# Sinkhorn-MoE behind banded attention: 1024-token blocks, with weight operands kept in DRAM after the first pass

## The chip, the cores and the metric

One core of a Trainium2 chip. The metric is device time in microseconds for one execution, the median of three runs. TensorE (PE) multiplies, VectorE (DVE), ScalarE (ACT) and GpSimd (POOL) work on its results and on its operands, and SyncE (SP) issues the DMA transfers.

## The reference

```python
scores = scale * np.matmul(q, k.transpose(0, 1, 3, 2)) + bias        # B 4, H 8, S 768, D 64
scores = np.where(keep, scores, -1000000000.0)                       # 8 global keys, 96 local
attn_out = softmax(scores) @ v
x = attn_out.transpose(0, 2, 1, 3).reshape(3072, 512)
P = np.exp(x @ w_gate - max)                                         # 8 experts
for _ in range(8):
    P /= P.sum(1, keepdims=True) + 1e-09
    P /= P.sum(0, keepdims=True) + 1e-09
    P *= N / E
for e in range(E):
    h = np.maximum(x @ w1[e], 0.0)                                   # w1[e]: 512 x 1024
    out += P[:, e:e + 1] * (h @ w2[e])                               # w2[e]: 1024 x 512
```

Every expert sees every token. All values are float32. The kernel writes a float32 operand as a high and a low part (`xh`, `xl`; `wh`, `wl`), so one product of 128 x 128 by 128 x n takes three matmuls: hi by lo, lo by hi, hi by hi.

## The kernel before

*Attention stage.* `Banded.unit` works on 8 units of 384 tokens, each with four head pairs, and leaves the result in `xh`, `xl` (the last write of a head pair is L390). Beside it runs a filler, `background`: the gate of a finished unit and its first `NF0 = 4` F-tiles (128 of the 1024 hidden columns each) of expert 0, by plain matmuls: layer 1 in `h_ps`, layer 2 in `y_ps`, whose result goes to `y_spill`. `between` doles it out over the attention's slots. The filler of the last unit comes after attention has ended, and `sinkhorn` is woven into it and the first steps.

*Block stage.* The remaining work is 30 groups, each two F-tiles of one expert, on four blocks of 768 tokens (two units each): 120 steps. `layer1_strassen` makes layer 1 of a block from seven products instead of eight, 42 matmuls 384 wide, in the banks `c`, `d`, `a`, `b`. `second` is layer 2, plain: 36 matmuls of 512 into `y_ps` for six token tiles, and for each tile a DVE operation (L944) that scales by the gate's weight `pm` and adds to `acc`. Layer 2 of a step stands in the program behind layer 1 of the next.

*Operands.* The seven token operands of a block (`right_operands`, `right_sums`, `right_difference`) are sums of x quarters; `combine` makes one with POOL (or POOL, DVE and ACT where `hurry` is set). The weight operands of a group are made once per half: SP loads `w1f` and `w2f` (512 KB each), POOL makes five sums `wsum` (L565), ACT copies the high parts (L542) and POOL subtracts the low ones (L543).

*Order.* The four blocks are worked in two halves of two, so all 30 groups' weights are prepared twice; x and the sums of the first two blocks wait in DRAM (`x_spill`, `s_spill`) and come back by `reload`. A scheduler orders the instructions of each engine, except where `keep_in_program_order` (class `InOrder`, L83, L86) holds PE's matmuls to the program: in attention, and in the block stage from the second expert on. All DMA transfers go through SP's queue.

## Time and profile before

| | us |
|---|---|
| median of three runs (2239.43 to 2240.81) | 2239.45 |
| profiled execution, first to last instruction | 2239.4 |
| PE busy | 2215.1 (99%) |
| DVE busy | 1388.3 (62%) |
| POOL busy | 791.7 (35%) |
| ACT busy | 693.3 (31%) |
| mean granted PE clock, share of full speed | 0.993 |
| moved by DMA | 133.74 MB, 60 GB/s over the span |

The span of the profiled execution is the device time within 0.1 us, so there is next to nothing around it. Busy shares are averages over two different stages: attention with filler up to about 340 us, and blocks from there to 2234. PE's durations overlap (a matmul's 0.4 us of 512 columns starts before the one ahead has ended), so work on PE is counted by starts.

### The profile page before, as it was taken

How to read it: one execution, taken by the hardware profiler on the slowest of the kernel's cores; microseconds unless marked ns; L12 is line 12 of the kernel's file. 1: busy time of each engine (PE TensorE's matmuls, PEld its weight loads, DVE VectorE, ACT ScalarE, POOL GpSimd, SP SyncE). 2: the span in 40 equal slices, each digit the busy share in tenths (PEclk: the TensorE clock that was granted, in tenths of full speed). 3: DMA queues.
4: the chain of work that ended last, by engine and by line, in shares of the span. 5: the costliest groups of instructions: out<-in, count | busy, mean ns of one | idle time of the engine just before them, and what ended most of it. 6: DMA issues, size and time to landing. Idle time of an engine off the chain costs nothing.

```text
span 2239.4 us, 31408 instructions
## 1 busy us (share of the span) xinstructions
PE 2215.1 (99%) x12147; PEld 1984.8 (89%) x12147; DVE 1388.3 (62%) x2682; ACT 693.3 (31%) x1592; POOL 791.7 (35%) x655
## 2 busy tenths in 40 slices
PE   8999999999999999999999999999999999999999
PEld 5888888989999899998999989989999899998997
DVE  5555557866666666666666666666666666666665
ACT  6677663232222222222222133222222222222221
POOL 5257356333333333323333234332333333333320
PEclk8999999999999999999999999999999999999999
DMA  7466432101101011010110551111011110111001
GB/s 167 127 181 170 120 97 66 37 30 38 38 29 34 33 38 38 29 38 29 38 38 29 188 188 39 38 30 37 29 39 38 34 33 29 38 38 38 29 20 58
DMA packets 177614, 133.74 MB, mean 60 GB/s; under 512 B 117040, under 2 KB 148784, under 8 KB 177456
## 3 DMA queue, kind: packets, MB, share of 16 engines
q1 hardware_dynamic: 177456, 131.65, 19.6%
q8 instruction: 97, 1.59, 0.3%
q14 instruction: 61, 0.50, 0.1%
HBM read 108.81 MB, written 22.81 MB: 59 GB/s over the span
## 4 chain that ended last, share of the span: by engine, by line
PE 92%; POOL 3%; ACT 2%; issue 2%; DVE 1%; DMA 0%; SPq 0%; ACTq 0%; DVEq 0%; POOLq 0%
PE y_ps L83 44%; PE bank_c L83 11%; PE bank_d L83 11%; PE bank_a L83 11%; PE bank_b L83 5%; PE h_ps L83 2%; PE t_ps L86 1%; PE s_ps L83 1%; PE o_ps L83 1%; PE tp L86 1%; ACT p_sb L296 1%; PE y_ps L690 1%; PE y_ps L692 0%; PE y_ps L691 0%; POOL xsum L615 0%
## 5 line engine op out<-in xcount | busy, mean ns | idle before, releaser
L944 DVE SCALAR_TENSOR_TENSOR acc<-y_ps,pm,acc 128x512 f32<-128x512 f32 x672 | 502.9, 748 | 260.7 <-PE y_ps L83 259.4
L83 PE MATMUL y_ps<-w2l,hh 128*128 128x512 f32 x1476 | 578.0, 392 | 0.0
L83 PE MATMUL y_ps<-w2h,hh 128*128 128x512 f32 x1476 | 576.9, 391 | 0.0
L83 PE MATMUL y_ps<-w2h,hl 128*128 128x512 f32 x1476 | 576.5, 391 | 0.0
L543 POOL TENSOR_TENSOR w2l<-w2f,w2h 128x1024 fp32r<-128x1024 f32 x60 | 144.4, 2406 | 646.6 <-ACT w2h L542 646.6
L83 PEld LDWEIGHTS y_ps<-w2h,hh 128*128 128x128 f32 x1476 | 276.9, 188 | 58.3
L83 PEld LDWEIGHTS y_ps<-w2h,hl 128*128 128x128 f32 x1476 | 277.1, 188 | 53.8
L83 PEld LDWEIGHTS y_ps<-w2l,hh 128*128 128x128 f32 x1476 | 277.2, 188 | 53.5 <-issue 0.2
L543 POOL TENSOR_TENSOR wl<-wsum,wh 128x1280 fp32r<-128x1280 f32 x60 | 177.9, 2964 | 350.6 <-ACT wh L542 350.6
L565 POOL TENSOR_TENSOR wsum<-w1f 128x256 f32<-128x256 f32 x300 | 213.4, 747 | 218.4 <-DMA w1f<-in_moe_w_dram 218.4
L630 ACT ACTIVATE hh<-bank_b 128x384 fp32r<-128x384 f32 x120 | 59.1, 492 | 399.8 <-DVE bank_b L670 396.2
L542 ACT CAST w2h<-w2f 128x1024 fp32r<-128x1024 f32 x60 | 63.2, 1053 | 380.9 <-PE y_ps L83 357.3
L663 ACT COPY t<-bank_c 128x384 f32<-128x384 f32 x120 | 57.8, 482 | 360.6 <-PE bank_c L83 353.9
L665 DVE TENSOR_TENSOR t<-t,bank_d 128x384 f32<-128x384 f32 x120 | 66.5, 554 | 165.6 <-PE bank_d L83 162.7
L83 PE MATMUL bank_c<-xh,wh 128*128 128x384 f32 x460 | 155.2, 337 | 0.0
L83 PE MATMUL bank_c<-xl,wh 128*128 128x384 f32 x460 | 154.9, 337 | 0.0
L83 PE MATMUL bank_c<-xh,wl 128*128 128x384 f32 x460 | 154.5, 336 | 0.0
L83 PE MATMUL bank_d<-xl,wh 128*128 128x384 f32 x460 | 153.8, 334 | 0.3 <-DVE hl L631 0.3
L83 PE MATMUL bank_d<-xh,wl 128*128 128x384 f32 x460 | 153.6, 334 | 0.0
L83 PE MATMUL bank_d<-xh,wh 128*128 128x384 f32 x460 | 153.6, 334 | 0.0
L83 PE MATMUL bank_a<-sl,wh 128*128 128x384 f32 x460 | 153.6, 334 | 0.0
L83 PE MATMUL bank_a<-sh,wl 128*128 128x384 f32 x460 | 153.6, 334 | 0.0
(219 smaller groups left out, 3986.6 us busy)
## 6 DMA issues: line engine op xcount, KB each, us to landing
w1f<-in_moe_w_dram SPq DMA_DIRECT2D x62, 512.0 KB, 3.5
w2f<-in_moe_w_dram SPq DMA_DIRECT2D x62, 512.0 KB, 3.6
out_dram<-acc SPq DMA_DIRECT2D x24, 256.0 KB, 2.2
ys<-y_sb SPq DMA_DIRECT2D x21, 256.0 KB, 2.1
acc<-ys SPq DMA_DIRECT2D x7, 768.0 KB, 5.1
acc<-in_q_dram SPq DMA_DIRECT2D x32, 96.0 KB, 2.6
acc<-in_k_dram SPq DMA_DIRECT2D x32, 96.0 KB, 2.5
acc<-in_v_dram SPq DMA_DIRECT2D x32, 96.0 KB, 2.3
```

The lines of the kernel that those rows point to most:

```text
L83: return self.tc.keep_in_program_order(self.engine.matmul(*args, **kw))
L86: return self.tc.keep_in_program_order(self.engine.transpose(*args, **kw))
L296: nc.scalar.activation(out=pv, in_=pv, func=AF.Exp, bias=mx[:, u:u + 1], scale=-1.0, accum_out=sm[:, i, j:j + 1])
L542: self.nc.scalar.copy(out=hi, in_=full)
L543: self.nc.gpsimd.tensor_tensor(out=lo, in0=full, in1=hi, op=ALU.subtract)
L565: nc.gpsimd.tensor_tensor(out=s[:, n], in0=x, in1=y, op=op)
L630: nc.scalar.activation(out=hh, in_=src, func=AF.Relu)
L663: nc.scalar.copy(out=t3, in_=c)
L665: tt(out=t3, in0=t3, in1=d, op=ALU.subtract)
L690: self.pe.matmul(y_ps, lhsT=hh[:, cols], rhs=lf, start=(f == 0), stop=False)
L944: nc.vector.scalar_tensor_tensor(out=a, in0=y_ps, scalar=moe.pm[:, tt, e:e + 1], in1=a, op0=ALU.mult, op1=ALU.add)
```

## The change

Blocks of 1024 tokens take the place of those of 768: three blocks, and every matmul of a block is 512 wide. `NF0` is 2, so the filler does the first two F-tiles of expert 0, and 31 groups are left. `layer1_fast` is a seven-product form with other sums (`FIRST`; four banks `x`, `y`, `z`, `w`).

Pass 1 works the third block while it makes the weights' operands. `make_group` makes for each group seven operands of w1 (four of them sums, `left_sums`) and seven of w2, and stores them in DRAM (`w1s`, `w2s`, 1.84 MB each). Layer 2 is plain there (48 matmuls).

Passes 2 and 3 work the first and second block. They make no weights: `load_first` and `load_second` read the operands back (`w1r`, `w2r`). Layer 2 has seven products too (`SECOND`, 42 matmuls into `m_ps`): class `Fast` scales the hidden values by the gate's weight (`pbc`, a row broadcast from DRAM), and makes the seven operands `hop` from them with POOL and ACT. The results of the products are added up over 29 groups in seven tiles `m` (128 x 1024) in SBUF by DVE (L1225), and are turned into output tiles once a pass: seven adds (L1229 to L1235), then in group 29 (`PLAIN`) 64 transposes in all `c_ps2` bring them to `acc` (L1253). The last two groups of a pass have layer 2 plain. The x operands of the first two blocks are stored as they are made, in pieces, and read by `load_x` (seven tiles of 1 MB, `xr`) ahead of a pass.

```diff
-NF0 = 4
+NF0 = 2
+HB = 4
+BT = 2 * HB
+BU = HB * P
+OPS = ("s1", "s2", "s3", "s4", "a11", "a12", "a22")
+FIRST = (("p1", "x", "a11", "b11", True), ("p6", "y", "s2", "t2", True), ("p2", "x", "a12", "b21", False),
+         ("p5", "z", "s1", "t1", True), ("p7", "w", "s3", "t3", True), ("p3", "z", "s4", "b22", False),
+         ("p4", "w", "a22", "t4", False))
+SECOND = (("p1", "a11", "b11"), ("p3", "s4", "b22"), ("p5", "s1", "t1"), ("p7", "s3", "t3"), ("p6", "s2", "t2"),
+          ("p2", "a12", "b21"), ("p4", "a22", "t4"))
...
-    def strassen_stage(self, e, f, stage):
...
+    def make_group(self, staged, pool, spool, stage, dst1, dst2, dst2p):
+
+        nc, KH, HD = self.nc, self.KH, self.DM // 2
+        s, w1f, w2f = staged
+        w = pool.tile([P, 7, 2, KH * P], F32R, name="w1ops")
+        v = pool.tile([P, FG * 2, 2, HD], F32R, name="w2ops")
+        self.split(w[:, 4:6, 0], w[:, 4:6, 1], w1f[:, :, 0:P].rearrange("p (o c) f -> p o c f", o=2))
+        self.split(w[:, 0:4, 0], w[:, 0:4, 1], s.rearrange("p o c f -> p o (c f)"))
+        self.split(w[:, 6, 0].rearrange("p (c f) -> p c f", f=P), w[:, 6, 1].rearrange("p (c f) -> p c f", f=P), w1f[:, KH:, P:])
+        for f, n in enumerate((slice(0, 4, 3), slice(1, 3))):
+            self.split(v[:, n, 0], v[:, n, 1], w2f[:, f].rearrange("p (e d) -> p e d", e=2))
+        nc.sync.dma_start(out=dst1.bitcast(F32), in_=w.bitcast(F32))
+        if dst2p is not None:
+            nc.sync.dma_start(out=dst2p.bitcast(F32), in_=v.bitcast(F32))
+        else:
+            s2 = stage.tile([P, 4, HD], F32, name="wsum2")
+            self.left_sums(s2, w2f[:, 0, 0:HD], w2f[:, 1, 0:HD], w2f[:, 0, HD:], w2f[:, 1, HD:])
+            sv = spool.tile([P, 4, 2, HD], F32R, name="s2ops")
+            self.split(sv[:, :, 0], sv[:, :, 1], s2)
+            nc.sync.dma_start(out=dst2[:, 4:7].bitcast(F32), in_=v[:, 0:3].bitcast(F32))
+            nc.sync.dma_start(out=dst2[:, 0:4].bitcast(F32), in_=sv.bitcast(F32))
...
+    def load_first(self, src, pool):
+        first = {}
+        for _, _, o, _, _ in FIRST:
+            n = OPS.index(o)
+            t = pool.tile([P, 2, self.KH, P], F32R, name="w1r")
+            self.nc.sync.dma_start(out=t.rearrange("p s c f -> p s (c f)").bitcast(F32), in_=src[:, n].bitcast(F32))
+            first[o] = t[:, 0], t[:, 1]
+        return first
...
-    def layer1_strassen(self, x, w, hpool, tmp, ps, tag):
...
+        for p, o, a, b, first in FIRST:
+            if first:
+                bank[o] = ps.tile([P, BU], F32, name=f"bank_{o}", tag="h")
+            self.products(bank[o], w[a], x[b], first, o == "y" or not first)
+            if p == "p1":
+                t = tmp.tile([P, BU], F32, name="t", bufs=2)
+                nc.scalar.copy(out=t, in_=bank["x"])
+            elif p == "p6":
+                tt(out=t, in0=bank["y"], in1=t, op=ALU.add)
+            elif p == "p2":
+                ended("b11", bank["x"])
+            elif p == "p5":
+                u4 = tmp.tile([P, BU], F32, name="u4")
+                tt(out=u4, in0=bank["z"], in1=t, op=ALU.add)
+            elif p == "p7":
+                tt(out=bank["y"], in0=bank["w"], in1=u4, op=ALU.add)
+                ended("b22", bank["y"])
+            elif p == "p3":
+                tt(out=bank["z"], in0=bank["z"], in1=t, op=ALU.add)
+                ended("b12", bank["z"])
+            else:
+                tt(out=bank["w"], in0=bank["w"], in1=t, op=ALU.add)
+                ended("b21", bank["w"])
...
+    def op(self, name, full):
+        t = self.o.tile([P, 2, BU], F32R, name="hop")
+        self.nc.scalar.copy(out=t[:, 0], in_=full)
+        self.nc.gpsimd.tensor_tensor(out=t[:, 1], in0=full, in1=t[:, 0], op=ALU.subtract)
+        self.ops[name] = t
+
+    def sum(self, name, x, y):
+        t = self.s.tile([P, BU], F32, name="hsum")
+        self.nc.gpsimd.tensor_tensor(out=t, in0=self.full[x], in1=self.full[y], op=ALU.subtract)
+        self.full[name] = t
+        self.op(name, t)
+
+    def ended(self, name, bank):
+        t = self.h.tile([P, BU], F32, name="h32")
+        self.nc.vector.scalar_tensor_tensor(out=t, in0=bank, scalar=0.0, in1=self.pbc[:, int(name[2]) - 1],
+                                            op0=ALU.max, op1=ALU.mult)
+        self.full[name] = t
+        if name in ("b11", "b22"):
+            self.op(name, t)
+        elif name == "b12":
+            self.sum("t1", "b12", "b11")
+            self.sum("t3", "b22", "b12")
+            self.sum("t2", "b22", "t1")
+        else:
+            self.op(name, t)
+            self.sum("t4", "b21", "t2")
...
 def pipeline(tc, attention, ident, moe, acc):
...
+        w1s = [dram.tile([P, 7, 2, KH * P], F32R, name=f"w1s{g}") for g in range(NG)]
+        w2s = [dram.tile([P, 7, 2, HD], F32R, name=f"w2s{g}") for g in range(PLAIN)]
+        w2p = [dram.tile([P, 2 * FG, 2, HD], F32R, name=f"w2p{g}") for g in range(PLAIN, NG)]
...
+        for g in range(NG):
+            if g > 0 and groups[g - 1][0] > 0:
+                moe.pe = attention.pe
+            hs, ended = plain_ops()
+            w = wts.pop(g)
+            make_next = g + 1
+
+            def each(n):
+                if n == 1:
+                    make(make_next)
+                steps(n)
+            together(moe.layer1_fast(x_ops, w[0], mps, ltmp, ended), prev, each)
+            w2 = w[1]
+            prev = second_plain(b, g, w2, hs, lambda k: yps.tile([P, DM], F32, name="y_ps", tag="y"),
+                                g == NG - 1, False)
...
+                def each(n, g=g):
+                    if n == 1:
+                        first_w[(g + 1) % NG] = moe.load_first(w1s[(g + 1) % NG], w1r) if g + 1 < NG or q + 1 < len(order) else None
+                two = pend.pop(0)
+                together(moe.layer1_fast(x_ops, w, mps, ltmp, ended), two, each)
...
+                    def second_fast(hs=hs, w2=w2, g=g, ms=ms):
+                        for p, a, o in SECOND:
+                            bank = mp.tile([P, 2, BU], F32, name="m_ps", tag="m")
+                            hh, hl = hs[o][:, 0], hs[o][:, 1]
+                            wt = w2[a]
+                            for d in range(2):
+                                ds = slice(d * P, (d + 1) * P)
+                                moe.pe.matmul(bank[:, d], lhsT=wt[:, 0, ds], rhs=hl, start=True, stop=False)
+                                moe.pe.matmul(bank[:, d], lhsT=wt[:, 1, ds], rhs=hh, start=False, stop=False)
+                                moe.pe.matmul(bank[:, d], lhsT=wt[:, 0, ds], rhs=hh, start=False, stop=True)
+                            if g == 0:
+                                ms[p] = mpool.tile([P, 2, BU], F32, name="m")
+                                nc.scalar.copy(out=ms[p], in_=bank)
+                            else:
+                                nc.vector.tensor_tensor(out=ms[p], in0=bank, in1=ms[p], op=ALU.add)
+                        if g == PLAIN - 1:
+                            tt = nc.vector.tensor_tensor
+                            tt(out=ms["p2"], in0=ms["p1"], in1=ms["p2"], op=ALU.add)
+                            tt(out=ms["p6"], in0=ms["p1"], in1=ms["p6"], op=ALU.add)
+                            tt(out=ms["p7"], in0=ms["p6"], in1=ms["p7"], op=ALU.add)
+                            tt(out=ms["p4"], in0=ms["p7"], in1=ms["p4"], op=ALU.add)
+                            tt(out=ms["p7"], in0=ms["p7"], in1=ms["p5"], op=ALU.add)
+                            tt(out=ms["p6"], in0=ms["p6"], in1=ms["p5"], op=ALU.add)
+                            tt(out=ms["p3"], in0=ms["p6"], in1=ms["p3"], op=ALU.add)
...
+                    def back(k, n, ms=ms):
+                        i, j = n % 2, n // 2
+                        t_ps = mp.tile([P, 2, BU], F32, name="c_ps2", tag="m")
+                        for d, p in enumerate(((("p2", "p4"), ("p3", "p7")))[i]):
+                            for c in range(2):
+                                moe.pe.transpose(out=t_ps[:, 0, (2 * d + c) * P:(2 * d + c + 1) * P],
+                                                 in_=ms[p][:, c, j * P:(j + 1) * P], identity=ident)
+                        nc.vector.tensor_tensor(out=acc[:, n], in0=t_ps[:, 0], in1=acc[:, n], op=ALU.add)
```

What this does to the order is seen at three places. On SP, in the steady stage of the block work before, loads of weights follow each other; a row is a transfer, the number behind a name its tile:

```order
L538 DMA w2f_6478<-in_moe_w2_dram 128x2x512
L537 DMA w1f_6737<-in_moe_w1_dram 128x4x256
L538 DMA w2f_6738<-in_moe_w2_dram 128x2x512
L537 DMA w1f_6997<-in_moe_w1_dram 128x4x256
L538 DMA w2f_6998<-in_moe_w2_dram 128x2x512
```

After, in pass 1, around the groups 23 to 25 (`w1s24` is the DRAM tile of group 24):

```order
L546 DMA w2f_8593<-in_moe_w2_dram 128x2x512
L597 DMA w2s22_253<-s2ops_8457 128x2048
L588 DMA w1s24_224<-w1ops_8763 128x3584
L545 DMA w1f_8916<-in_moe_w1_dram 128x4x256
L597 DMA w2s23_254<-s2ops_8619 128x2048
L596 DMA w2s23_254<-w2ops_8602 128x1536
L546 DMA w2f_8755<-in_moe_w2_dram 128x2x512
L588 DMA w1s25_225<-w1ops_8925 128x3584
L545 DMA w1f_9078<-in_moe_w1_dram 128x4x256
L596 DMA w2s24_255<-w2ops_8764 128x1536
L546 DMA w2f_8917<-in_moe_w2_dram 128x2x512
L597 DMA w2s24_255<-s2ops_8781 128x2048
```

Each load of `w1f` now stands behind a store of `w1ops`, and the load of `w2f` behind one store of a w2 operand or behind two, in turn.

On PE before, the end of a step's layer 1 (`bank_a`) and the first layer 2 matmuls of the step ahead:

```order
L83 MATMUL bank_a<-sl_5124,wh 128x384
L83 MATMUL bank_a<-sh_5123,wl 128x384
L83 MATMUL bank_a<-sh_5123,wh 128x384
L83 MATMUL y_ps<-w2l,hh 128x512
L83 MATMUL y_ps<-w2h,hl 128x512
```

After, in pass 2 at the change from group 28 to 29 (a row with x6 is one product; `ident` marks the transposes):

```order
L92 MATMUL bank_z<-xr,w1r 128x512 x6
L92 MATMUL m_ps<-hop,w2r 128x512 x6
L92 MATMUL bank_w<-xr,w1r 128x512 x6
L92 MATMUL m_ps<-hop,w2r 128x512 x6
L92 MATMUL bank_x<-xr,w1r 128x512 x6
L92 MATMUL y_ps_15309<-w2r,hop 128x512 x6
L95 MATMUL c_ps_15317<-ident,m 128x128 x4
L92 MATMUL bank_y<-xr,w1r 128x512 x6
L92 MATMUL y_ps_15309<-w2r,hop 128x512 x6
L95 MATMUL c_ps_15338<-ident,m 128x128 x4
```

The two layers now alternate product by product in program order, and the first transposes come two products after the last `m_ps`.

On DVE before, one step's layer 1 and the additions of layer 2:

```order
L665 TENSOR_TENSOR t_13085<-t_13085,bank_d 128x384
L668 TENSOR_TENSOR h_13100<-bank_a,t_13085 128x384
L670 TENSOR_TENSOR bank_b<-bank_b,h_13100 128x384
L631 SCALAR_TENSOR_TENSOR hl<-bank_b,hh 128x384
L673 TENSOR_TENSOR t_13085<-bank_d,t_13085 128x384
L674 TENSOR_TENSOR t_13085<-t_13085,bank_c 128x384
L676 TENSOR_TENSOR bank_a<-bank_a,t_13085 128x384
L944 SCALAR_TENSOR_TENSOR acc<-y_ps,pm,acc 128x512
```

After, at the same place of pass 2 as above:

```order
L1229 TENSOR_TENSOR m<-m 128x1024
L1225 TENSOR_TENSOR m<-m_ps,m 128x1024
L1234 TENSOR_TENSOR m<-m 128x1024
L667 SCALAR_TENSOR_TENSOR hop<-bank_w,hop 128x512
L1094 SCALAR_TENSOR_TENSOR acc<-y_ps_15309,pm,acc 128x512
L1232 TENSOR_TENSOR m<-m 128x1024
L1235 TENSOR_TENSOR m<-m 128x1024
L1233 TENSOR_TENSOR m<-m 128x1024
L1253 TENSOR_TENSOR acc<-c_ps_15317,acc 128x512
```

Behind the last addition of a product (L1225), four of the seven adds of whole `m` tiles stand ahead of the operation that takes the first transposed tile.

More of the change, by code (lines that the diff above doesn't have):

```diff
@@ L616, in combine @@
             nc.gpsimd.tensor_tensor(out=dst[1], in0=s, in1=dst[0], op=ALU.subtract)
-    def products(self, out, hi, lo, xhi, xlo, n, first, last):
-        nc = self.nc
-        for c in range(n):
-            self.pe.matmul(out, lhsT=hi(c), rhs=xlo(c), start=(first and c == 0), stop=False, skip_group_check=True)
-            self.pe.matmul(out, lhsT=lo(c), rhs=xhi(c), start=False, stop=False, skip_group_check=True)
-            self.pe.matmul(out, lhsT=hi(c), rhs=xhi(c), start=False, stop=(last and c == n - 1), skip_group_check=True)
@@ new lines, in products @@
+    def products(self, out, w, x, first, last):
+        (hi, lo), (xh, xl) = w, x
+        for c in range(self.KH):
+            self.pe.matmul(out, lhsT=hi[:, c], rhs=xl[:, c], start=(first and c == 0), stop=False, skip_group_check=True)
+            self.pe.matmul(out, lhsT=lo[:, c], rhs=xh[:, c], start=False, stop=False, skip_group_check=True)
+            self.pe.matmul(out, lhsT=hi[:, c], rhs=xh[:, c], start=False, stop=(last and c == self.KH - 1),
+                           skip_group_check=True)
@@ new lines, in layer2 @@
+    def layer2(self, n, w, hs, y_ps):
+        i, j = n % 2, n // 2
+        cols = slice(j * P, (j + 1) * P)
+        w2h, w2l = w
+        for f in range(FG):
+            h = hs[f"b{f + 1}{i + 1}"]
+            hh, hl = h[:, 0, cols], h[:, 1, cols]
+            wf, lf = w2h[f], w2l[f]
+            self.pe.matmul(y_ps, lhsT=hh, rhs=lf, start=(f == 0), stop=False, skip_group_check=True)
+            self.pe.matmul(y_ps, lhsT=hl, rhs=wf, start=False, stop=False, skip_group_check=True)
+            self.pe.matmul(y_ps, lhsT=hh, rhs=wf, start=False, stop=(f == FG - 1), skip_group_check=True)
@@ new lines, in pipeline, with run @@
+        opens = [((n - 1) // UT + 1) * slots + LAG for n in bounds[1:]]
+        closes = opens[1:] + [NU * slots]
+        halves = [((h * HB + HB - 1) // UT + 1, h) for h in range(TT // HB - 1)]
+        todo = [[o, max(c, o + 1), cost(nt), chunk(b, t0, nt), 0, b] for (b, t0, nt), o, c in zip(chunks, opens, closes)]
+        now = [0]
+        def run(part, until):
+            while part[3] is not None and part[4] < until:
+                step = next(part[3], None)
+                if step is None:
+                    part[3], part[4] = None, part[2]
+                else:
+                    part[4] += step
@@ L869, in pipeline @@
                 spill(len(spills))
[L870 removed]
+            x = segments(u)
             if u == NU - 1:
[L872 to L873 removed]
+                staged = moe.stage_group(*groups[0], stage)
+            attention.unit(u, x, between)
             if u == 0:
@@ L970, in pipeline @@
-        second(*prev)
+        wpools.append(mid.enter_context(tc.tile_pool(name="wpool1", bufs=1, side="right", reuse_waits="tile")))
+        views = [x.rearrange("p c (j i q) -> p c i j q", i=2, q=P) for x in xs[b]]
+        x_ops = {f"b{k + 1}{i + 1}": tuple(v[:, k * KH:(k + 1) * KH, i] for v in views) for k in range(2) for i in range(2)}
+        x_ops |= {o: (t[:, 0], t[:, 1]) for o, t in ops[b].items()}
+        for n in range(TT // HB):
+            if n // 2 == b and n % 2 == 0:
+                nc.sync.dma_start(out=acc[:, 0:HB], in_=y_spill[n])
@@ new lines, in together @@
+        def together(one, two, each=None):
+            one, two = [x if x is not None else iter(()) for x in (one, two)]
+            n, done = 0, [False, False]
+            while not all(done):
+                for i, it in enumerate((one, two)):
+                    if not done[i]:
+                        try:
+                            next(it)
+                        except StopIteration:
+                            done[i] = True
+                if each is not None:
+                    each(n)
+                n += 1
@@ new lines, in pipeline @@
+        for _ in sinkhorn:
+            pass
+        for _ in turned:
+            pass
+        moe.pe = attention.pe
+        tail = prev
+        pend = [tail]
+        mid.close()
+        early.close()
+        raise_ = None
+        xr = top.enter_context(tc.tile_pool(name="xr", bufs=8, reuse_waits="tile"))
+        mpool = top.enter_context(tc.tile_pool(name="mpool", bufs=7, side="right", reuse_waits="tile"))
+        w2r = top.enter_context(tc.tile_pool(name="w2r", bufs=8, side="right", reuse_waits="tile"))
```

572 lines of the change are left out of this document (320 added, 252 removed).

## The prediction

> **What bounds the kernel now.** I read the page's busy line and chain first, then the windows by stage, then single rows.
>
> ```profile
> PE 2215.1 (99%) x12147; PEld 1984.8 (89%) x12147; DVE 1388.3 (62%) x2682; ACT 693.3 (31%) x1592; POOL 791.7 (35%) x655
> PE 92%; POOL 3%; ACT 2%; issue 2%; DVE 1%; DMA 0%; SPq 0%; ACTq 0%; DVEq 0%; POOLq 0%
> core 0: us, PE busy (x) PEld busy (x) DVE busy (x) ACT busy (x) POOL busy (x), PEclk, DMA share, GB/s
> 20.00:57.00 37.00, 30.98 (x258) 25.48 (x258) 21.82 (x84) 29.13 (x98) 17.54 (x15) 0.79 0.81 198
> 57.00:336.00 279.00, 276.04 (x2308) 236.93 (x2309) 149.80 (x527) 195.09 (x595) 136.76 (x75) 0.99 0.52 139
> 336.00:375.00 39.00, 35.34 (x188) 30.73 (x187) 28.40 (x39) 15.51 (x28) 30.11 (x19) 0.98 0.28 89
> 375.00:2234.00 1859.00, 1858.61 (x9331) 1683.89 (x9329) 1176.07 (x1981) 446.78 (x855) 596.71 (x522) 1.00 0.13 44
> ```
>
> TensorE is busy 99% of the span, and the chain runs through it for 92%. In the block stage (375 to 2234) it is never free at clock 1.00, with DVE at 63%, POOL at 32%. In the attention stage (57 to 336), attention and filler share it at 99%, ACT at 70%. Only ahead of 57, where no filler runs yet, is it not full. So matmuls taken away shorten the kernel one for one, until another engine or the DMA becomes the bound. The price of a matmul is its pitch, start to start, since the durations overlap:
>
> ```profile
> 899.80 0.40 PE L83 MATMUL y_ps<-w2h,hh 128*128 128x512 f32 x1
> ...
> 907.54 0.33 PE L83 MATMUL bank_c<-xl,wh 128*128 128x384 f32 x1
> ...
> 914.85 0.39 PE L83 MATMUL y_ps<-w2l,hh 128*128 128x512 f32 x1
> ```
>
> Between the first two rows lie 34 starts of 128x512 in 7.74 us: 0.2276 us each. Between the last two lie 42 of 128x384 in 7.31 us: 0.174. A step before (42 and 36) is 15.50 us; 120 steps are 1860.
>
> **Block matmuls.** After, every block matmul is 512 wide. Pass 1: 31 groups of 42 + 48. Passes 2 and 3: 29 groups of 42 + 42, two of 42 + 48. That is 2790 + 5232 = 8022, times 0.2276 = 1826 us. The 64 fp32 transposes that bring the sums back have no like row; between 0.06 (a quarter of a 512-wide pitch) and 0.23 they cost 4 to 15; I take 7, nearer the narrow end since each is 128 wide. Together 1833, 27 less than before.
>
> **Attention.** Filler goes from four F-tiles to two.
>
> ```profile
> 57.00:336.00 279.00, 71.33 (x336) 56.23 (x336) 15.52 (x28) 13.75 (x28) 0.99 0.52 139
> 57.00:336.00 279.00, 63.66 (x228) 39.77 (x229) 0.00 (x0) 10.55 (x19) 0.99 0.52 139
> 35.08 0.55 DVE L390 TENSOR_TENSOR xl<-o_ps,xh 128x384 fp32r<-128x384 f32 x1
> ...
> 57.26 0.56 DVE L390 TENSOR_TENSOR xl<-o_ps,xh 128x384 fp32r<-128x384 f32 x1 [1.48 <-ACT xh L389]
> L390 DVE TENSOR_TENSOR xl<-o_ps,xh x32: 547/557/559, 35.1 to 339.8; 128x384 fp32r<-128x384 f32 x32
> ```
>
> The first two rows are the filler alone: h_ps (336 matmuls, 58.5 us by pitch), then y_ps (228 recorded; the code gives 7 x 36 = 252, 57.4 us). Half of 116 goes: 58 us. Would attention by itself take the place? Head pairs end at 35.1 and, the fourth, at 57.3, with no filler: 7.4 us each, although half clock fell into it. The remaining 28 at that pace need 207 us, and 282.5 - 58 leaves 224. ACT's 195 us lose half of the hh and y_sb work (12): 183 in 224, 82%. I therefore let all 58 show: the last xl lands at 282, between 264 (all at the unfilled pace) and 310 (half is lost).
>
> **From attention to blocks.** Before, 339.8 plus gate and filler of the last 384 tokens (8 x 0.174 + 48 x 0.174 + 36 x 0.2276 = 17.9), plus 1860 and a tail of 5.4 (its row is below), make 2223 of 2239.4: 16 us are holes, half clock and small matmuls here. After, gate and filler are 56 matmuls of 512, 12.7 us. For the rest I take 14, as before and a little less: the second product of the first group needs t2, and only the filler and the first product (1.4) stand ahead of it, 14 us. In that time POOL has three xres and the first group's splits to do, some 13 us at the prices below, and DVE behind each xres three operations of the kind that POOL holds up: t2 is 2 to 6 us late. Bounds: 5, and 28 (a whole half's sums on POOL, 20 x 1.3, that nothing covers).
>
> ```profile
> 370.17 2.36 POOL L543 TENSOR_TENSOR w2l<-w2f,w2h 128x1024 fp32r<-128x1024 f32 x1
> 370.28 2.47 DVE L759 TENSOR_TENSOR pm<-pm,csum 128x192 f32<-128x192 f32 x1
> L759 DVE TENSOR_TENSOR pm<-pm,csum 128x192 f32<-128x192 f32 x8 | 5.0, 624 | 0.2
> 374.00 0.69 PE L622 MATMUL bank_c<-xl,wh 128*128 128x384 f32 x1 [2.77 <-DVE hl L631]
> 373.30:380.10 6.80, 6.10 (x18) 5.81 (x19) 5.52 (x13) 1.74 (x4) 3.60 (x5) 0.50 0.30 80
> 44.20:45.60 1.40, 0.23 (x5) 0.03 (x2) 0.52 (x1) 1.13 (x3) 1.01 (x1) 1.00 0.71 218
> 45.60:52.40 6.80, 6.56 (x36) 5.43 (x36) 3.92 (x15) 4.45 (x14) 2.51 (x4) 0.50 1.05 272
> ```
>
> These rows show two things that the sum needs. A DVE operation whose two inputs are both in SBUF was held to the end of POOL's (2.47 us where eight average 0.62). And a hole costs twice: after 2.77 us, and even after 1.4 (44.2 to 45.6), the clock stands at 0.50 for 6.8 us, which loses 3.4. The Trainium skill ("TensorE: Matmul & The Clock Gate", Part 1) has the array throttled only after an idle window of about 3.4 us. By it a hole of 1.4 us would cost itself alone, about 7 us less in the whole sum, 2168; the trace disagrees, and I go by the trace.
>
> **Pass 1: the weights.** Per group POOL makes seven operands of each layer, SP stores them and then loads the next group.
>
> ```profile
> L565 POOL TENSOR_TENSOR wsum<-w1f 128x256 f32<-128x256 f32 x300 | 213.4, 747 | 218.4 <-DMA w1f<-in_moe_w_dram 218.4
> L543 POOL TENSOR_TENSOR w2l<-w2f,w2h 128x1024 fp32r<-128x1024 f32 x60 | 144.4, 2406 | 646.6 <-ACT w2h L542 646.6
> L542 ACT CAST wh<-w1f 128x256 fp32r<-128x256 f32 x120 | 42.5, 401 | 0.0
> w1f<-in_moe_w_dram SPq DMA_DIRECT2D x62, 512.0 KB, 3.5
> 370.25 0.37 SPq L537 DMA_DIRECT2D w1f<-in_moe_w_dram  x1
> GB/s 152 5 0 150 0 0 0 5 0 150 0 1 149 0 5 0 0 16 334 358 423 414 182 2 150 248 358 416 432 413 405 382 123 210 174 294 245 130 0 0
> ```
>
> A 512-wide POOL operation is put between the two rows: 0.747 + 256 x 2.16 ns = 1.30 us. Per group: 8 sums of 256 (6.0), splits of 2406 twice, 1.30 three times, 0.75 once: 15.4 us beside 90 matmuls of 20.5. POOL fits. The loop does not fit so clearly. The store of w1ops (1.84 MB, 4.3 us at the 432 GB/s of the last row, the reload at 1190 to 1330) goes ahead of the next w1f on the same queue: 0.4 to issue, 4.3, 3.5 to land, 8.2. Then come four sums (3.0), the four of w2 (3.0) and three splits (4.5), each behind a copy by ACT (0.4 that shows): 19.1 us. Where both stores of w2 stand ahead of the w2f load, the longer one (1.05 MB, 2.4) joins the loop: 21.5. The two kinds alternate in the queue; the mean, 20.3, is just under 20.5. I take 6 us over the pass, between 0 and 45 (every period 21.9).
>
> **Passes 2 and 3.** POOL has 11 operations of 1.30: 14.3 in 19.1 us.
>
> ```profile
> L940 DVE TENSOR_TENSOR acc<-y_ps,acc 128x512 f32<-128x512 f32 x48 | 32.7, 682 | 13.6 <-PE y_ps L83 10.1 <-PE y_ps L692 3.3
> L665 DVE TENSOR_TENSOR t<-t,bank_d 128x384 f32<-128x384 f32 x120 | 66.5, 554 | 165.6 <-PE bank_d L83 162.7
> L944 DVE SCALAR_TENSOR_TENSOR acc<-y_ps,pm,acc 128x512 f32<-128x512 f32 x672 | 502.9, 748 | 260.7 <-PE y_ps L83 259.4
> 2233.97 0.75 DVE L944 SCALAR_TENSOR_TENSOR acc<-y_ps,pm,acc 128x512 f32<-128x512 f32 x1 [0.61 <-PE y_ps L83]
> ys<-y_sb SPq DMA_DIRECT2D x21, 256.0 KB, 2.1
> out_dram<-acc SPq DMA_DIRECT2D x24, 256.0 KB, 2.2
> ```
>
> DVE has seven adds of m_ps, 1024 wide: twice 0.682 is 1.36; by the slope from 384 to 512, 1.0 ns an element, 1.19. Seven of 1.2, five of 0.68 and four of 0.75 make 14.8, at most 15.9. All of these have an input in PSUM, and such operations kept their price beside POOL (L944: 748 on average through the whole stage). Loads: 3.67 MB a group, 192 GB/s. All under 19.1, so TensorE stays the bound and these edits cost nothing beside their matmuls; what covers them is 3 to 5 us of slack a group. Turning to a new block loads seven x tiles of 1 MB, 17.7 us at 415 GB/s, as far as its first group's matmuls reach; I take 4 us for both, of 0 to 15.
>
> Group 29 of each pass (PLAIN) ends the seven sums: seven adds of 1024 with SBUF operands on both sides stand on DVE ahead of the first transposes. DVE reaches the last one some 7.7 us after the last m_ps product, TensorE is through its next twelve matmuls in 2.7: a wait of 5 us. Each c_ps2 then shares two buffers with y_ps2, about 0.5 us eight times. With half clock behind it (3.4, above), 12; I take 9 a pass, 18 in all, because POOL may release more, between 6 and 32. The Trainium skill ("SBUF — State Buffer", Who interferes with whom) holds DVE operations with two SBUF inputs against GpSimd reads as an exclusive lock, which the L759 row bears out; by it each of the seven could wait for a POOL operation of 1.3 more, 9 us a pass, and the sum would be 2193. I leave it at the upper end, because POOL has made the last fast group's operands by then.
>
> **The sum.** 282 + 12.7 + 14 + 1833 + 6 + 4 + 18 = 2169.7; the tail (from the start of the last L944, 2234.0, to the end of the span, 2239.4: the last store) adds 5.4: 2175. The profiled span of before is 2239.4, its median 2239.45, so no correction is needed. That is 2.9% faster.
>
> **Rivals.**
> - *The weight loop paces pass 1.* Every group takes the 21.5 and 0.4 of landing, 21.9 instead of 20.5: 31 x 1.4 = 43, less the 6 counted: 2212. For it: load, sums and store are one chain, and 4.7 MB a group is 231 GB/s where the block stage moved 44. Against: POOL's own work is 15.4.
> - *Attention does not follow.* The x operands of two blocks are written in smaller pieces, and SP issues them one after the other; if half of the 58 is lost, 2204. For it: before 57, at DMA share 0.81, TensorE had gaps at a pace that is hardly faster. Against: 224 us is still over the 207.
> - *Slower.* The same loop at a price not seen here: stores to DRAM beside loads at half of the reload's rate. The store of w1ops takes 9 us, and the first kind of period 23.8, the second 28.6; even 24 for all is 31 x 3.5 = 108 on top: 2277. It decides from 20.5 + 64/31 = 22.6 us a group up. Against: the 256 KB stores of ys and out land 2.1 to 2.2 us after issue, under a load's 3.5 for twice the size.
> - *Nothing of note.* Half of attention's gain lost and the loop at 21.9: 2241, inside 0.2%, which is about what a measurement of this kernel can tell from no change.
> - *Better.* All waits hidden and attention at the unfilled pace: 2140.
>
> **Chances.** Forecast 0.54 (2150 to 2195 holds it), loop 0.17, attention 0.13, better 0.05, nothing 0.03, slower 0.08. Faster by more than 0.2%: 0.89. The range goes from 2136 to 2224.
>
> **What would show it.** TensorE at 97% or more after 300 us. Pass 1's groups 20.5 us apart, and POOL about 75% busy there; if 21.5 or more, TensorE idles ahead of each bank_x for w1ops, and the weight rival is right. The last xl near 282. Passes 2 and 3 19.1 us apart, idle only at group 29. Above 2224 I would look first at w1s landing times. The forecast is wrong where POOL's waits come from DMA, or where DVE, not TensorE, is released last in pass 2.

## The result, and the profile after

The changed kernel takes 2207.3 us (median of four runs, 2205.98 to 2211.06) against 2239.44 before: a ratio of 0.9857, 95% interval 0.9843 to 0.9871. It is 1.4% faster, half of the 2.9% that was forecast. The profiled span is 2204.2 us, 1.8 under its own run's time, so the forecast of 2175, a sum of spans, is missed by 29 us. Every later run shows such a gap, of 1.7 to 2.0 us; the 0.1 us read ahead of the prediction set one execution's span beside the median of three, so "no correction is needed" was off by about 2 us.

The page's busy line and chain, after:

```profile
PE 2129.7 (97%) x10507; PEld 1741.8 (79%) x10507; DVE 1493.0 (68%) x2286; ACT 752.3 (34%) x1579; POOL 1411.1 (64%) x1197
PE 83%; ACT 5%; DVE 4%; POOL 3%; DMA 2%; issue 2%; SPq 0%; DVEq 0%; ACTq 0%; POOLq 0%
```

The windows by stage, after: attention, pass 1, pass 2, the end of pass 2 (the header stands with the prediction):

```profile
57.00:322.00 265.00, 233.44 (x2021) 182.74 (x2019) 143.06 (x520) 189.35 (x590) 129.21 (x101) 0.99 0.60 159
414.00:954.00 540.00, 539.25 (x2381) 446.21 (x2380) 317.63 (x453) 181.91 (x299) 381.56 (x356) 1.00 0.62 230
988.00:1545.00 557.00, 554.79 (x2447) 458.78 (x2445) 417.11 (x461) 148.81 (x248) 395.53 (x314) 1.00 0.73 212
1545.00:1612.00 67.00, 60.99 (x269) 49.20 (x270) 36.83 (x53) 16.37 (x25) 15.20 (x12) 0.95 0.76 268
```

Attention's last operation, in the view of one line (its first and last start):

```profile
L399 DVE TENSOR_TENSOR xl<-o_ps,xh x40: 280/552/559, 35.2 to 321.9; 128x384 fp32r<-128x384 f32 x24, 128x256 fp32r<-128x256 f32 x8, 128x128 fp32r<-128x128 f32 x8
```

The block passes came as forecast: TensorE is free for 0.75 us of 540 in pass 1 and for 2.2 of 557 in pass 2, with POOL at 71% in both. The view of L399 has attention's last `xl` at 321.9 us where 282 was forecast, and the first of the windows has TensorE at 88% there. All that follows 321.9 took 1882 us, against the 1893 that the forecast gave it. So attention alone is 40 us over, and the rest 11 under.

The chain of waits in attention shows the difference. Before, in order of time (start, length, what):

```profile
196.76 0.44 PE tp L86 x4
197.20 0.90 PE s_ps L83 x12
198.11 1.02 PE o_ps L83 x16
199.13 0.81 PE t_ps L86 x6
199.94 2.63 PE h_ps L83 x15
202.56 0.22 PE tp L86 x2
```

After, at the same time:

```profile
195.80 0.45 PE tp L95 x4
...
196.28 0.60 ACT kh L253
...
196.90 0.70 DVE kl L254
...
197.64 0.66 PE s_ps L92 x6
198.30 0.06 DVE p_sb L301
...
199.77 0.37 ACT p_sb L305
...
200.35 0.47 ACT acc L327
200.82 0.50 ACT p_sb L305 x2
201.32 0.48 ACT pT L327
201.80 0.04 issue
201.84 0.55 PE tp L95 x3
```

Before, the chain never leaves TensorE, and `h_ps` (filler) is a link of it. After, it runs round the engines: keys turned by TensorE, copied by ACT (`kh`), their low part by DVE (`kl`), scores on TensorE (`s_ps`), DVE, exponentials on ACT (L305), the copies of the turned weights among these (L327: `acc` and `pT`), and TensorE again. The longest of TensorE's waits in attention (57 to 322 us), after:

```profile
PE r_ps L95 <- ACT acc L327: 13.0, 19, 1.3
PE s_ps L92 <- DVE kl L254: 6.2, 10, 0.9
PE tp L95 <- ACT pT L327: 3.5, 8, 0.5
```

Two theories were tried first. One-for-one theory (the forecast's): TensorE bounds attention, so what is taken off TensorE comes off the time. Cover theory: attention has a floor of its own, this chain, and the filler had hidden it; then half the filler saves less than half of its time. A third, traffic, blames the smaller x pieces and their stores.

### The profile page after: what moved, and what is told of

Same layout as the page of the kernel before. It is cut to its first block, busy times and chain, and to the rows that moved or that the text cites. A ratio compares the mean times of both kernels' runs of the same rounds, so it can differ in the third digit from the quotient of the medians.

```text
span 2204.2 us, 31207 instructions
## 1 busy us (share of the span) xinstructions
PE 2129.7 (97%) x10507; PEld 1741.8 (79%) x10507; DVE 1493.0 (68%) x2286; ACT 752.3 (34%) x1579; POOL 1411.1 (64%) x1197
## 4 chain that ended last, share of the span: by engine, by line
PE 83%; ACT 5%; DVE 4%; POOL 3%; DMA 2%; issue 2%; SPq 0%; DVEq 0%; ACTq 0%; POOLq 0%
PE m_ps L92 25%; PE y_ps L92 15%; PE bank_z L92 11%; PE bank_w L92 11%; PE bank_x L92 11%; PE bank_y L92 5%; ACT p_sb L305 2%; PE s_ps L92 1%; DMA w2f<-in_moe_w_dram 1%; PE o_ps L92 1%; PE tp L95 1%; POOL wsum L567 1%; POOL w1ops L551 1%; PE t_ps L95 1%; PE h_ps L92 1%
## 5 line engine op out<-in xcount | busy, mean ns | idle before, releaser
L92 PE MATMUL m_ps<-hop,w2r 128*128 128x512 f32 x2436 | 618.2, 389 | 0.5 <-issue 0.5
L1225 DVE TENSOR_TENSOR m<-m_ps,m 128x1024 f32<-128x1024 f32 x392 | 478.3, 1220 | 187.5 <-PE m_ps L92 184.8
L92 PEld LDWEIGHTS m_ps<-hop,w2r 128*128 128x128 f32 x2436 | 457.1, 188 | 95.8 <-issue 0.9
L824 POOL TENSOR_TENSOR hop<-h,hop 128x512 fp32r<-128x512 f32 x174 | 226.5, 1302 | 333.4 <-ACT hop L823 333.2
L92 PE MATMUL y_ps<-w2ops,hop 128*128 128x512 f32 x1344 | 336.8, 389 | 0.0
L824 POOL TENSOR_TENSOR hop<-hsum,hop 128x512 fp32r<-128x512 f32 x232 | 296.1, 1301 | 4.5 <-ACT hop L823 4.5
L1094 DVE SCALAR_TENSOR_TENSOR acc<-y_ps,pm,acc 128x512 f32<-128x512 f32 x256 | 191.6, 749 | 155.2 <-PE y_ps L92 154.1
L92 PEld LDWEIGHTS y_ps<-w2ops,hop 128*128 128x128 f32 x1344 | 252.3, 188 | 52.3
L92 PE MATMUL bank_x<-xr,w1r 128*128 128x512 f32 x744 | 189.2, 390 | 0.1
L92 PE MATMUL bank_z<-xr,w1r 128*128 128x512 f32 x744 | 189.2, 390 | 0.0
L305 ACT ACTIVATE p_sb<-p_sb,mx 128x256 f32<-128x256 f32 (+1 forms) x192 | 92.4, 484 | 52.2 <-DVE mx L301 52.2
```

What stands on the lines that cost most here:

```text
L92: return self.tc.keep_in_program_order(self.engine.matmul(*args, **kw))
L305: nc.scalar.activation(out=pv, in_=pv, func=AF.Exp, bias=mx[:, u:u + 1], scale=-1.0, accum_out=sm[:, i, j:j + 1])
L824: self.nc.gpsimd.tensor_tensor(out=t[:, 1], in0=full, in1=t[:, 0], op=ALU.subtract)
L1094: nc.vector.scalar_tensor_tensor(out=a, in0=y_ps, scalar=moe.pm[:, tt, e:e + 1], in1=a, op0=ALU.mult, op1=ALU.add)
L1225: nc.vector.tensor_tensor(out=ms[p], in0=bank, in1=ms[p], op=ALU.add)
```

## The experiments

A time without a ratio beside it is that of one run.

**Half the filler in the kernel before** (`-NF0 = 4`, `+NF0 = 2`).

> The kernel before with NF0 = 2 instead of 4 and nothing else: half the filler, 31 groups, 124 steps (62 us more of blocks). Cover theory (attention has waits of its own, the filler only covered them, and half of it covers less): the last xl moves from 339.8 to 305-325 only, TensorE is below 93% busy from 57 us to there, and the time is 2265 to 2287. One-for-one theory (the prediction's: TensorE bounds attention): the last xl lands at 280-287, TensorE stays at 98%, and the time is about 2245. Traffic theory (it is the smaller x pieces and their stores of the changed kernel that hold attention up): as one-for-one, since this kernel has none of them.

2266.4 us. The view of the line that ends a head pair:

```profile
L390 DVE TENSOR_TENSOR xl<-o_ps,xh x32: 546/558/562, 35.2 to 308.5; 128x384 fp32r<-128x384 f32 x32
```

The window of attention:

```profile
57.00:310.00 253.00, 232.26 (x2058) 186.44 (x2058) 145.25 (x517) 189.63 (x585) 136.97 (x76) 1.00 0.57 153
```

From the first to the last `xl`, 304.7 us became 273.3: 31 saved of some 58 us of matmuls. TensorE is at 92%. There is no new piece or store in this kernel, so this loss is not traffic. It is not one-for-one either.

**No filler matmuls in attention** in the changed kernel. It leaves out the filler's products and stores zeros in their place.

```diff
+            if dst is None:
+                for t in range(nt):
+                    y_sb = fy.tile([P, DM], F32, name="y_sb")
+                    nc.vector.memset(y_sb, 0.0)
...
+                return
             for w in ws:
```

> The changed kernel without the filler's matmuls during attention: the first 20 tiles of expert 0's first two F-tiles are left out, zeros are stored in their place; gate, x pieces, stores and all later stages stay. Cover theory: attention keeps its own pace, some 7.4 us a head pair as before 57 us, so the last xl lands at 262-290, not lower; TensorE falls under 75% there. Traffic theory: POOL, SP or the DMA queue set the pace, and the last xl stays at 310-322. One-for-one theory: 55 us less matmuls, 267, with TensorE's waits unchanged at some 33 us.

2212.7 us, with the last `xl` at 328.5 and the first, by a slower start, at 43.0: 285.5 us between them, where the changed kernel with all its filler takes 286.7. Some 55 us of matmuls fewer saved nothing. TensorE's waits there:

```profile
PE r_ps L95 <- ACT acc L327: 21.7, 21, 5.3
PE s_ps L92 <- DVE kl L254: 10.9, 12, 4.2
PE tp L95 <- ACT acc L327: 9.1, 10, 1.2
PE tp L95 <- ACT pT L327: 7.3, 17, 0.6
```

And the window:

```profile
57.00:310.00 253.00, 186.70 (x1654) 143.51 (x1653) 136.60 (x509) 170.66 (x547) 113.57 (x91) 0.91 0.63 162
```

The same waits grew. From 57 to 310 us TensorE was free for 66.3 us, where it was free for 31.6 in the changed kernel: 35 of the 55 us became idle time. The granted clock fell to 0.91, which lengthens the matmuls that are left. The 328.5 lies outside all three expectations. That for the cover theory, 262 to 290, was too low because it still used the pace of 7.4 us a pair, and the start was 8 us later than with the filler, which no run explains.

**Little x traffic.** One POOL sum and one store per half block are kept.

```diff
-                for o in ("b11", "b21", "b22"):
+                for o in ():
...
-                for o in ("t3", "t1", "t2", "t4"):
+                for o in ("t3",):
```

> The changed kernel with most of the x traffic of attention left out: for the first two blocks only one of four sums is made by POOL (5 of 20 operations per half block), and one of sixteen stores per half block is issued; passes 2 and 3 read that one tile in place of all seven (so their x is not the reference's). Traffic theory: the last xl moves from 321.9 to 280-295 and the time to 2167-2180. Cover theory: the last xl stays at 312-322 and the time at 2197-2207.

2201.1 us, last `xl` at 317.6. With the filler beside it, traffic costs at most some 4 us of the 40 (282.6 us from first to last `xl`, in place of 286.7). That is little more than the difference between two builds: in the run with later transposes below, attention is the same program, and its last `xl` came 3.5 us later.

**Neither filler nor traffic.** Both edits together, to see the floor bare.

> The changed kernel without the filler's matmuls in attention (zeros are stored instead) and with most of the x traffic left out (one of four POOL sums and one of sixteen stores per half block; passes 2 and 3 read that one tile for all seven): attention with little beside it. If the prediction's floor was right (7.4 us a head pair, read ahead of 57 us, where there is neither filler nor traffic), and only traffic made it longer, 31 pairs take 229 to 240 us from the first xl to the last. If the floor itself was mis-sized (the pace ahead of 57 us is that of one kind of unit, and the chain over the engines takes some 9 us a pair in the steady stage), 265 to 285, as in the two runs without filler that kept the traffic (274.7 and 285.5).

2201.2 us. The view of the line, then the window:

```profile
L399 DVE TENSOR_TENSOR xl<-o_ps,xh x40: 280/557/559, 44.1 to 317.3; 128x384 fp32r<-128x384 f32 x24, 128x256 fp32r<-128x256 f32 x8, 128x128 fp32r<-128x128 f32 x8
```

```profile
57.00:310.00 253.00, 191.15 (x1765) 147.60 (x1767) 144.59 (x537) 179.04 (x574) 45.95 (x36) 0.94 0.47 114
```

273.2 us for 31 head pairs: 8.8 us each with almost nothing beside them, where 7.4 was read. POOL is at 18% and ACT at 71%, TensorE at 76%: no engine is full. The floor itself had been mis-sized.

Two cautions. The granted clock was 0.94 here, so part of the 8.8 is half clock. An estimate from that figure is at most 0.06 x 253 = 15 us of the stretch, which would leave 8.3 a pair (28 pairs would still need 233 us, more than 224). But half the filler in the kernel before, at clock 1.00, took 273.3 us as well: there, 58 us of filler matmuls cost nothing over the bare stage. And without filler the traffic counts for more than with it: 285.5 us against 273.2.

**The order of scores and transposes.**

```diff
-            self.ahead(range(t + AHEAD, t + AHEAD + CHUNK))
             self.flush()
             turned = [(t + c, self.turn(t + c)) for c in range(CHUNK)]
+            self.ahead(range(t + AHEAD, t + AHEAD + CHUNK))
```

> The changed kernel with one swap in the attention loop: the scores of the slots ahead are issued behind the value products and the transposes of the present slots, not ahead of them. Ring theory (without enough filler attention is bound by a chain that closes over the engines once per two slots: keys transposed on PE, copied by ACT, their low part by DVE, scores on PE, minimum on DVE, exponentials on ACT, the copy of the transposed weights queued behind these on ACT, and PE's next transposes behind that copy): the swap puts 2 us of PE work between the low part of the keys and the scores, and the copy ahead of the exponentials; PE's waits for the low part of the keys (11.1 us) and for the copy (13.0 and 3.5) go mostly, the last xl moves from 321.9 to 295-310 and the time to 2180-2196. Engine theory (ACT at 71%, with DMA at 0.6, is as busy as it can be): the waits move elsewhere, the last xl stays at 316-325.

2201.9 us, ratio to before 0.9832 (0.9816 to 0.9849). From the first `xl` (31.7) to the last (316.1) are 284.4 us; more than half of the gain is an earlier start. TensorE's waits moved:

```profile
PE t_ps L95 <- DVE kl L254: 13.4, 17, 1.5
PE o_ps L92 <- DMA acc<-in_v_dram: 6.6, 5, 2.3
```

TensorE waits for the same `kl`, now at the transposes: `tp`, `t_ps` and `r_ps` share two PSUM buffers (tag `tp`), and `kl` is what last reads one of them. The waits of `r_ps` for L327 in the changed kernel are of that kind too. A third buffer was not tried. As an improvement this fell short of the 295 to 310 that the ring theory (the chain above) expected; 316.1 is the lower edge of what the engine theory gave.

> The same swap in the kernel without the filler's matmuls during attention (that kernel's last xl was at 328.5 with its first at 43.0, 285.5 us for 31 head pairs, no faster than with the filler). Ring theory: the chain is all there is, and it gets shorter by the part that the swap takes out: 285.5 becomes 225-265. Engine theory: within 5 us of 285.5.

2194.5 us, 34.1 to 308.8: 274.7 us in place of 285.5. The chain got 10.8 us shorter, more than the engine theory's 5, but it did not come down to the ring theory's 225 to 265.

**The copy of the transposed weights on DVE** (`-self.nc.scalar.copy(`, `+self.nc.vector.tensor_copy(` at L327).

> The changed kernel with the copy of the transposed weights out of PSUM done by DVE instead of ACT (some 190 copies of 0.35 to 0.69 us change engines). Ring theory: the copy no longer queues behind ACT's exponentials, PE's waits of 13.0 and 3.5 us for it shrink, last xl 300-318. Engine theory with ACT as the limit: ACT loses some 45 us of 189, last xl 285-295. If DVE's own queue is as long: 320-330.

2194.2 us in one run, 35.2 to 312.3: 277.1 us, 10 less. TensorE's waits for that copy went from 13.0 and 3.5 us to 3.2 and 1.7 (view of the waits):

```profile
PE r_ps L95 <- DVE acc L327: 3.2, 7, 0.8
PE tp L95 <- DVE acc L327: 1.7, 3, 1.1
```

The window of attention:

```profile
57.00:310.00 253.00, 228.84 (x1976) 181.56 (x1970) 184.79 (x594) 150.78 (x499) 129.11 (x101) 0.98 0.63 165
```

ACT went from 71% to 60% and DVE from 54% to 73%, and the chain got shorter. The copy of 128x512 itself takes longer on DVE (0.68 us against 0.57 on ACT, means from 57 to 310 us), so the gain is not a shorter copy. What fits is its place in a queue: on DVE it does not stand behind the exponentials. ACT's load as the limit had asked for 285 to 295; that did not come, but the edit changes load and queue together, so a share of the load is not ruled out.

The same edit in the kernel before:

> The kernel before, with the copy of the transposed weights on DVE and nothing else. Cover theory: with four F-tiles TensorE is 99% busy in attention and no chain over the other engines shows, so the last xl stays at 337-341 and the time within 3 us of 2239.5. If a chain over ACT paced attention there too, the last xl moves by the 10 us that it moved in the changed kernel, to 330 or lower, and the time to 2230.

2236.1 us in one run, 33.4 to 335.0: 301.6 us in place of 304.7. With TensorE at 99%, the edit is worth 3 us where it was worth 10, as the cover theory has it, and half of the 3 lies in the first unit (20.7 us for three pairs in place of 22.2), where no filler runs yet. The last `xl` lies a little under the 337 to 341 I gave, mostly since the start is 1.7 earlier.

**Four F-tiles again** in the changed kernel. To make room, filler tiles, hidden buffers and pieces are smaller, attention's `inv` has two buffers instead of three, and the filler's slots are set by hand.

```diff
-NF0 = 2
+NF0 = 4
...
-            last = ((b + 1) * BT if (b + 1) * BT - t <= HB else t + (UT if b == 0 else HB))
-            bounds.append(last)
+            bounds.append(t + 2)
...
         fill.close()
+        make(0)
```

> The changed kernel with four F-tiles of filler again, as before the change (one group less; to make room, the filler works two token tiles at a time, hidden buffers are half as long, two x pieces instead of three, and the first group's operands are made behind the last filler). Cover theory: attention without filler takes about as long as with two F-tiles, so of the 55 us of matmuls that come back into it, 15 to 30 show: last xl at 337-352. Blocks lose a group of 258 matmuls (58.7 us), the filler behind attention grows by 11, the late first operands cost about 5: 2172 to 2196 in all. One-for-one theory: last xl at 375-380 and the time 2215 to 2222, since the group that goes is worth what the filler costs.

2211.5 us, ratio 0.9866 (0.9850 to 0.9883): 4 us more than the changed kernel, between the two forecasts. The last `xl` at 356.8 means that 55 us of matmuls cost 33.5 from first to last `xl` (320.2 against 286.7): a little over the 15 to 30 of the cover theory, and well under one-for-one. The smaller buffers are in this figure too. Of the group's 58.7 us, 28 show behind the last `xl`. The rest went into the longer filler there and into waits that the changed kernel does not have. Two of them are 6.1 us at 497 and 5.4 at the turn to pass 2. At 497 TensorE waits for the copy `t` (L698), which stands on ACT behind copies of w2's operands; these wait for POOL's sums, and POOL for the landing of `w2f`, until 491.8. At the turn it waits for a load of `w2r`. Why these loads came late is open.

**More slots for the last filler** (`-[NU * slots]`, `+[NU * slots + 36]`).

> The changed kernel with the last piece of filler in attention (four token tiles in 18 slots) doled out over 54 slots, so that most of it is left for behind attention. If uneven filler is why the changed kernel's attention (286.7 us from first to last xl) takes 13 us longer than the old one's with the same two F-tiles (273.3), the last unit's 34.6 us become about 29, last xl 315-318, and what is left over costs 7 us behind attention, where TensorE is full: total 2205 to 2211. If the last units are long for another reason (x pieces of the third block, sums on POOL), the last unit stays over 33 us and the total grows to 2212 or more.

2218.5 us: the last `xl` moved to 317.3, the last unit from 34.6 to 27.0 us, but behind attention TensorE then waits 8.5 us for the Sinkhorn steps and runs at clocks of 0.91 to 0.97. Neither expectation came whole: the last `xl` is that of the first, the total that of the second. That the filler doled out over the last unit lengthens it by 7.6 us is shown; that uneven filler accounts for all of the 13 us between 273.3 and 286.7 is not. By units (four head pairs each, from `xl` to `xl`), 11 of the 13 stand in the last two: they take 41.1 and 34.6 us in the changed kernel, 35.1 and 29.4 in the kernel before with half the filler. The last but one stays long with little traffic (40.7) and with neither traffic nor filler (38.9), and why is open.

**The store of w1's operands issued twice.**

```diff
         nc.sync.dma_start(out=dst1.bitcast(F32), in_=w.bitcast(F32))
+        nc.sync.dma_start(out=self.twice.bitcast(F32), in_=w.bitcast(F32))
```

> The changed kernel with the store of each group's first-layer operands (1.84 MB) issued twice in pass 1, the second time to a tile that nobody reads: a test of how far the weight loop is from setting the pace. My loop of 19.1 and 21.5 us a group, whose mean was just under the matmuls' 20.5, gets 4.3 us longer: 23.4 and 25.8, mean 24.6 in place of 20.4, 125 us more in pass 1 (about 2330). If the loop has slack that I did not count (the next group's load goes out a group earlier than I thought), less than 1 us a group (under 2240).

2207.6 us, no change. DMA in the changed kernel (the first two rows: the transfers of one tile, and the window from 430 to 950), and the same here:

```profile
w1s<-w1ops SPq DMA_DIRECT2D x25, 1792.0 KB, 6.8
```

```profile
430.00:950.00 520.00, 519.25 (x2291) 429.79 (x2290) 304.38 (x434) 171.55 (x280) 368.80 (x346) 1.00 0.62 230
```

```profile
twice<-w1ops SPq DMA_DIRECT2D x26, 1792.0 KB, 10.7
```

```profile
430.00:950.00 520.00, 518.54 (x2288) 429.05 (x2287) 305.57 (x435) 173.86 (x280) 367.24 (x346) 1.00 0.84 323
```

At 323 GB/s and 0.84 of the DMA engines, TensorE is still free for only 1.5 us of 520. The loop I had built from store, load, sums and splits is not closed that tightly.

**Group 29's transposes two tiles later.**

```diff
                     def back(k, n, ms=ms):
+                        for m in ORDER[k - 2:k - 1] if 2 <= k < BT - 1 else ORDER[BT - 3:] if k == BT - 1 else []:
+                            back_one(m, ms)
+
+                    def back_one(n, ms):
                         i, j = n % 2, n // 2
```

> The changed kernel with the transposes of group 29 moved two tiles later in program order (tile k's sums are brought back behind tile k+2's products, the last three together). If the wait of 5.97 us ahead of the first transposes and the half clock behind it are what group 29 costs, both go: 8 to 10 us less in each of the two passes, 2187 to 2192. If another wait takes their place (the two buffers shared by transposes and products, or the same adds two tiles later): 2 us a pass at most, 2203 to 2207.

2200.6 us, ratio 0.9828 (0.9811 to 0.9844): 6.7 less. Attention, which the edit does not touch, took 3.5 us more in this build; behind the last `xl` it is 9 us less, 4.6 a pass. In the changed kernel, the timeline at the place:

```profile
1541.68 1.21 DVE L1229 TENSOR_TENSOR m<-m 128x1024 f32<-128x1024 f32 x1
...
1543.95 1.21 DVE L1234 TENSOR_TENSOR m<-m 128x1024 f32<-128x1024 f32 x1
...
1547.47 1.22 DVE L1235 TENSOR_TENSOR m<-m 128x1024 f32<-128x1024 f32 x1
1548.61 1.22 DVE L1233 TENSOR_TENSOR m<-m 128x1024 f32<-128x1024 f32 x1
1548.83 0.66 PE L95 MATMUL c_ps<-ident,m 128*128 128x128 f32 x2 [5.97 <-DVE m L1235]
```

The window behind that hole:

```profile
1549.00:1556.00 7.00, 6.61 (x22) 5.07 (x22) 2.83 (x4) 0.00 (x0) 0.00 (x0) 0.59 0.28 83
```

And TensorE's longest wait in the edited kernel, from 330 us on:

```profile
PE y_ps L92 <- DVE acc L1094: 9.5, 9, 2.3
```

The 5.97 us are gone, but a y tile then waits 2.25 for its buffer, because L1094 stands behind the same adds on DVE. The time lies between the two expectations.

**The edits that gained, together.**

> The changed kernel with two edits: group 29's transposes later, and the copy of the transposed weights on DVE. Alone they gave 6.7 and 13 us. They lie in different stages, so they should add up: 2185 to 2190. If the one run of the copy was a lucky order of the scheduler, 2192 to 2200.

2185.1 us (2181.1 to 2186.5), ratio 0.9749 (0.9733 to 0.9766): the fastest kernel of this study, with the last `xl` at 310.2. The gains of two stages add up.

> The changed kernel with two F-tiles and all three edits that gained alone: transposes of group 29 later (-6.7), the copy of the transposed weights on DVE (-13), the scores behind the transposes (-5.4). If the copy and the swap take out different waits, they add up: 2180 to 2186. If both take out the same wait of PE for the copy, the swap adds nothing: 2186 to 2190. PE's waits in attention do not go to zero in either case, as values wait for v (8 us of DMA waits in the run with the copy on DVE).

2192.0 us, ratio 0.9777 (0.9761 to 0.9794): the swap on top is a loss, worse than either expectation. TensorE waits 15.7 us for `kl` there.

> As the run with four F-tiles of filler, and with the transposes of group 29 two tiles later (6.7 us less when done alone) and the copy of the transposed weights on DVE (13 us less when done alone, its last xl at 312.3). If the copy's gain was a shorter chain in a stage that TensorE did not fill, it is worth less here, where TensorE is nearly full: 3 to 8 us, so 10 to 15 below the run without the two. If it was ACT's load that paced attention whatever the filler, the full 13 and 6.7: 20 below.

2188.1 us, ratio 0.9762 (0.9746 to 0.9779), 23 less than with four F-tiles alone, last `xl` at 343.2. That is more than the two edits gave alone (20), which is what I had expected if ACT's load paced attention whatever the filler; for the shorter chain I had expected 10 to 15. In attention, 320.2 us became 306.8: the copy was worth 13 here, 10 in the changed kernel and 3 in the kernel before, with TensorE at 94%, 88% and 99% without the edit. So its worth does not fall evenly as TensorE fills. This run does not separate ACT's load from its queue either.

## Why the prediction was right or wrong

- *What bounds it, and the pitch*: right for the blocks. Once pass 1 is steady, the period of a group is 20.2 to 20.6 there for all but a few (20.5 forecast), and it is 19.04 in passes 2 and 3 (19.1), by the copy behind each first product. The pitch is 19.04 / 84 = 0.2267 instead of 0.2276, which makes 7 us over the 8022 matmuls:

```profile
662.83 0.58 ACT L698 COPY t<-bank_x 128x512 f32<-128x512 f32 x1
683.06 0.59 ACT L698 COPY t<-bank_x 128x512 f32<-128x512 f32 x1 [0.22 <-PE bank_x L92]
...
1084.59 0.59 ACT L698 COPY t<-bank_x 128x512 f32<-128x512 f32 x1 [0.64 <-PE bank_x L92]
1103.62 0.59 ACT L698 COPY t<-bank_x 128x512 f32<-128x512 f32 x1 [0.65 <-PE bank_x L92]
```

- *Attention*: wrong, and more than the whole of the miss. The step that failed is "The remaining 28 at that pace need 207 us": a pace of 7.4 us a pair, read over three pairs of the first unit, ahead of 57 us. That is no sample of the stage: in the kernel before with half the filler, where these three pairs take 7.3 each, the units behind take 9.7 and 8.8 a pair in turn. With neither filler nor traffic the stage takes 8.8. At that pace the 28 pairs need 246 us, more than the 224 that TensorE's matmuls leave, so 57 + 28 x 8.8 = 303 would have been the bound, and "I therefore let all 58 show" falls with it. This is about half of the 40 us. Of the 19 from 303 to 321.9, up to 4 are x traffic. The others stand mostly in the last two units, where the filler's doling is a part; the split is open. The upper bound of 310 was exceeded too.
- *The rival "attention does not follow"* gave 2204, and the measured time is 2207. Its number is near by luck: attention lost 40 us where the rival lost 29, and the blocks gave 11 back. Its reason, SP's small stores, was not the cause: nearly all stores gone moved attention by 4 us.
- *Passes 2 and 3 cost nothing beside their matmuls*: right. L1225 took 1.22 us where 1.2 was put, POOL's 512-wide operation 1.30 as interpolated.
- *The weight loop*: 6 us allowed, about none seen in the steady part, and its rival and the slower case are refuted by the doubled store. The landing of `w1s` (6.8 us, 4.3 counted) was longer, yet hidden.
- *Group 29*: 9 us a pass forecast. In pass 2 the step takes 34.2 us between its copies where 90 matmuls and 32 transposes (0.36 us for four) need 20.4 + 2.9: 11 a pass. The wait was 5.97 where 5 was put. The half clock came as forecast: 0.59 over the 7 us behind that hole. The Trainium skill ("TensorE: Matmul & The Clock Gate", Part 1) ties it to an idle window of about 3.4 us. The hole of 5.97 agrees with that; the 2.25 us ahead of a y tile in the kernel with later transposes, with a clock of 0.72 over the next 6 us, do not. The lock of the Trainium skill's "SBUF — State Buffer" (Who interferes with whom) did not show and could not: POOL does nothing in that stretch, and the adds ran at 1.21.
- *Turns between passes*: 4 us allowed; TensorE is free for none at the first and for at most 1.4 at the second (0.84 and 0.54, between 1593 and 1604).

## What to carry to other kernels

Work that fills the waits of a chain hides the chain's length, so what is saved by taking it out ends where the chain's own length begins. Read that floor in the steady stage, or measure it with the filler left out; a first unit is not the steady stage. In such a stage, moving one copy to another engine's queue can be worth more than removing tens of microseconds of matmuls: 10 us here, where 55 us of matmuls fewer saved none. With TensorE at 99% the same edit gave 3.

## What was not expected of the hardware

TensorE kept its 20.4 us a group while stores and loads together moved 323 GB/s, though transfers took long to land: a `w2f` of 512 KB took 3.6 us in the kernel before at 35 GB/s, 8.6 in the changed kernel at 230, and 11.5 here (one of `w1f`: 3.4, 7.9 and 6.6). And a stage with all matmuls of the filler gone ran at a granted clock of 0.91 instead of 0.99, though the waits shown above are about 1 us each on average: taking work off TensorE slowed what was left.
